# Retention and bilinear FFN on one core: the q product of slots 13, 15, 17 and 19 as eight copies each on ScalarE instead of one on GpSimd

## The chip, the cores and the metric

The kernel runs on one core of a Trainium2 chip. The metric is device time in microseconds (us) from launch to end; the lower the better. The engines are named as the profile names them: PE is TensorE (matmuls; PEld is its weight load), ACT is ScalarE, DVE is VectorE, POOL is GpSimd, and SP is SyncE, from which nearly all transfers are issued. Each engine works through its own instructions in order; between engines, semaphores say when data or a buffer is ready.

## The reference

What is computed is a retention layer (linear attention with a decay per head) followed by a bilinear feed-forward network:

```python
def _attn_ref(q, k, v):                      # (4, 8, 768, 64) each
    B, H, S, D = q.shape
    gamma = 1.0 - 2.0 ** (-5.0 - np.arange(H, dtype=np.float32))
    scale = 1.0 / np.sqrt(D)
    state = np.zeros((B, H, D, D), dtype=np.float32)
    y = np.zeros_like(q)
    for t in range(S):
        state = gamma[None, :, None, None] * state + np.einsum('bhd,bhe->bhde', k[:, :, t], v[:, :, t])
        y[:, :, t] = scale * np.einsum('bhd,bhde->bhe', q[:, :, t], state)
    return y

def _moe_ref(x, w_a, w_b, w_out):            # x: 3072 tokens x 512; w_a, w_b: 512 x 1536; w_out: 1536 x 512
    return ((x @ w_a) * (x @ w_b)) @ w_out
```

The output is float32, 3072 x 512.

## The kernel before

The 3072 tokens are cut into 24 *slots* of 128 tokens (4 batches of 6 slots). The decay is taken out of the recurrence: k of token n and head h is multiplied by a factor from a table (`ktab`), q by its inverse with the scale (`qtab`), and what is left is causal attention without a softmax, with a running state per batch. The function `scaled(eng, t, i)` makes this product for slot t, with i = 0 for k and i = 1 for q. It reads the float32 tile that a transfer has brought (`kf`, `qf`, 128 tokens x 8 heads x 64) and writes bfloat16 into the tile `kqb` of the slot. The product is one instruction of 128 x 512 (line 292), with the table's column per head broadcast over 64.

`casts(t)` prepares one of the slots 8 to 19: a new `kqb` tile, the k product, then whatever `between` holds, the q product, in slots 8 to 11 the cast of v, and then `flip(t)`, a transposing transfer issued on SP that turns `kqb` into `kqT`, followed by the loads of a later slot. q of two slots (t even and t+1) comes in one transfer. v of slots 12 to 23 is cast on ACT by `v_cast` (line 249).

Two slots after another, `turn` does the attention on PE, and the result, copied into `xt` by ACT (line 431), goes into the feed-forward network. The network runs in groups J of 2 slots (256 tokens; group 5 has 4 slots). In a *block* `ffn_ab(J, ft)` PE makes `a` (four matmuls, line 568), ACT copies it out of PSUM as `asb` (line 571), PE makes `g` (four matmuls, line 580), and DVE multiplies g by asb into `ht` (line 582). There are 12 blocks a group, numbered by ft. The PSUM banks for a and g come from a ring of three (tag "ff"), in rotation: a bank is free once its copy on ACT (an a) or its product on DVE (a g) has been made.

The output product of a group is made by a Strassen-like scheme, `Group`: its steps `p1` to `p7` (line 685) accumulate into banks A, B and C, and between steps ACT takes snapshots of A (`snaps`, line 692), before the next product goes on to add to A, and DVE adds a snapshot to B or C. The sums of `ht` that the scheme needs (`hs`, line 618) are made on POOL. `single` weaves one such group with the blocks 0, 1 and 2 of the next: p1, p7, p2, block 0, p6, block 1, p5, block 2, p3, p4. `laced` does the same for group 4 and the products of group 5 (`fa`, `fb`, with snapshots `snapf`, line 961).

The order on each engine is the order in which the program is written: `seq` chains each instruction to the one before it on its engine. The main part around the change reads, in words: slot 13 is prepared after the blocks of group 2 and before `single(2)`; slot 14 after `single(2)`; slot 15 after the blocks 3 to 5 of group 3 and before block 6; slots 16 and 17 before and after `single(3)`, slot 17 thus ahead of the casts of v of slot 14 and of the blocks 3 and 4 of group 4; slots 18 and 19 within and after group 4, slot 19 just before `laced`.

Of the kernel before, what the change touches and what calls it, by code (L numbers as in the profile page):

```python
# [31 lines left out]
def kernel(  # L32
# [10 lines left out]
    nc = tc.nc  # L43
    P = 128
    B, H, S, D = q.shape
    NCH = S // P
    HP = H // 2
# [55 lines left out]
    def seq(bi):  # L103
        ins = bi.ins
        prev = last.get(ins.engine)
        if prev is not None:
            tc.add_manual_dep(ins, prev.name, nosync, reason="program order")
        last[ins.engine] = ins
        return bi
# [7 lines left out]
    def load_slot(t, names="kqv"):  # L117
        b, ci = divmod(t, NCH)
        for nm in names:
            src = {"k": k, "q": q, "v": v}[nm]  # L120
            if nm == "q":
                if t % 2 == 0:
                    load_two(nm, src, b, ci // 2, t)
                continue
            if t % 2 == 0:
                whole[nm] = raw_tile([P, 2, H, D], F32, nm + "f", nm + "f")
            raws[nm, t] = whole[nm][:, t % 2]
            s = src[b, :, ci * P : (ci + 1) * P, :].rearrange("h p d -> p h d")
            seq(nc.sync.dma_start(out=raws[nm, t], in_=s))
# [117 lines left out]
    def cast(engine, dst, src):  # L247
        if engine is nc.scalar:
            seq(nc.scalar.copy(dst, src))
        else:  # L250
            seq(engine.tensor_copy(dst, src))  # L251
# [29 lines left out]
    def scaled(eng, t, i):  # L281
        tab = tabs[0] if i else tabs[1 if t < 2 * PAIRS else 2]
        dst, src, tab = kqb[t][:, i], raws["kq"[i], t], tab[:, t % NCH]
        if t < 2 * PAIRS:
            dst, src = (x.rearrange("p (hp r) d -> p hp r d", r=2) if x is src else x
                        for x in (dst, src))
            tab = tab.rearrange("p (hp r) o -> p hp r o", r=2).to_broadcast([P, HP, 2, D])
        else:
            dst = dst.rearrange("p hp r d -> p r hp d")
            src = src.rearrange("p (r hp) d -> p r hp d", r=2)  # L290
            tab = tab.rearrange("p (r hp) o -> p r hp o", r=2).to_broadcast([P, 2, HP, D])
        seq(eng.tensor_tensor(dst, src, tab, op=ALU.mult))  # L292

    def new_nat(t):
        kqb[t] = nat.tile([P, 2, HP, 2, D], BF16, tag="kqb", name="kqb")
        kb[t], qb[t] = kqb[t][:, 0], kqb[t][:, 1]
        vb[t] = nat.tile([P, H, D], BF16, tag="vb", name="vb")

    def casts(t, between=lambda: None):
        new_nat(t)  # L300
        scaled(nc.gpsimd, t, 0)
        between()
        scaled(nc.gpsimd, t, 1)
        if t not in range(12, 20):
            cast(nc.gpsimd, vb[t], raws["v", t])
        u = t + 2
        if u == 20:
            load_slot(u, "kq")
        flip(t)
        if u == 20:  # L310
            load_slot(u + 1, "k")
            return
        if u == 21:
            load_slot(u - 1, "v")
            load_slot(u, "v")
            load_slot(22, "kq")
            return
        if u in V_LATE:
            if u == 13:
                load_slot(12, "q")  # L320
            elif u == 19:
                load_slot(18, "kq")
            load_slot(u, {12: "k", 18: ""}.get(u, "kq"))
            if u % 2:
                load_slot(u - 1, "v")
                load_slot(u, "v")
        elif u < NSLOT:
            load_slot(u)

    def flip(t):  # L330
        if t % 2 == 0:
            kqT[t // 2] = tra.tile([P, 2, 2, HP, P], BF16, tag="kqT", name="kqT", bufs=3)
        seq(nc.sync.dma_start_transpose(
            out=kqT[t // 2][:, t % 2].rearrange("p a b c -> p (a b) c"),
            in_=kqb[t].rearrange("p a hp r d -> p (a hp r d)")))

    def late_kq(t):
        for u in (t, t + 1):
            new_nat(u)
            scaled(nc.gpsimd, u, 0)  # L340
            scaled(nc.gpsimd, u, 1)
            flip(u)
        if t == 20:
            load_slot(23, "k")
            load_slot(22, "v")
            load_slot(23, "v")
# [803 lines left out]
    ffn_out(0, 1, 1)  # L1150
    weight_sum(4)
    casts(8)
    weight_pieces(2)
    ffn_out(0, 2, 0)
# [4 lines left out]
    ffn_out(0, 3, 0)  # L1159
    ffn_out(0, 3, 1)  # L1160
    casts(9)
    weight_pieces(2)
    turn(None, 6)
    single(1, AT0, AT1, FF)
    casts(10)
    weight_pieces(4)
    casts(11)
# [101 lines left out]
```

## Time and profile before

| | before |
|---|---|
| median of 3 runs | 218.36 us (218.28 to 218.38) |
| span of the profiled execution, first to last instruction | 216.57 us |
| PE busy | 210.7 us |
| POOL busy | 154.2 us, 184 instructions |
| DVE busy | 147.5 us, 272 instructions |
| ACT busy | 104.9 us, 235 instructions |
| granted clock of PE | 1.00 |

The profile is of one execution; its span leaves out what lies before the first and after the last instruction, so the runs' times stand 1.79 us above it. In the timelines below a row gives the start and the duration in us, the engine, the line of the program, the operation, the output and the inputs by the program's names, the shape, how many instructions the row merges, and in square brackets the idle time of the engine just before, with what ended it. In the groups, the numbers behind the count are busy us, mean ns of one, and the idle time before them. In the chain of waits, shares of the span are given by the engine on which the work that ended last lay. In the rows by stage, each engine's busy time is followed by its count of instructions.

### The profile page before, as it was taken

To read this page: it belongs to the slowest core of one execution; us is meant where nothing else is said; L and a number is where in the kernel's file an instruction comes from. 1 tells how busy PE (TensorE), PEld (TensorE's weight loads), DVE (VectorE), ACT (ScalarE), POOL (GpSimd) and SP (SyncE) were. 2 spreads that over 40 slices of the span, in tenths; PEclk is the share of its full clock that TensorE was granted. 3 is DMA by queue.
4 is the path that set the end of the run, shared out by engine and by line. 5 is a ranking of instruction groups with operands and counts; after the bars stand their busy time and mean duration, and the time that the engine had idled before them with its cause. 6 is when DMAs were issued, how large, how long until landed. Compare 5 with 4: busy or idle time off the path is not lost.

```text
span 216.6 us, 5713 instructions
## 1 busy us (share of the span) xinstructions
PE 210.7 (97%) x2252; PEld 146.1 (67%) x2252; DVE 147.5 (68%) x272; ACT 104.9 (48%) x235; POOL 154.2 (71%) x184
## 2 busy tenths in 40 slices
PE   7889999999999999999999999999999999999994
PEld 3557445587458888888888877457864444458883
DVE  3777346845984486356377978676577987688962
ACT  3256325343224444464576475657546656652331
POOL 5265876879878678969869979899986999530000
PEclk9999999999999999999999999999999999999999
DMA  5999999999999999999979999950013000000055
GB/s 162 290 320 365 387 311 360 384 268 232 221 264 227 228 231 222 158 192 269 197 169 245 222 209 234 236 127 3 5 69 125 2 0 3 2 0 0 27 194 170
DMA packets 85162, 39.68 MB, mean 183 GB/s; under 512 B 57488, under 2 KB 78864, under 8 KB 85136
## 3 DMA queue, kind: packets, MB, share of 16 engines
q1 hardware_dynamic: 84992, 39.26, 76.8%
q8 instruction: 17, 0.28, 0.5%
q14 instruction: 9, 0.07, 0.1%
q10 hardware_dynamic: 144, 0.07, 0.1%
HBM read 28.31 MB, written 6.29 MB: 160 GB/s over the span
## 4 chain that ended last, share of the span: by engine, by line
PE 91%; SPq 3%; DMA 3%; POOL 0%; issue 0%; DVE 0%
PE a L568 18%; PE g L580 18%; PE mA L685 12%; PE uA L859 10%; PE mB L685 6%; PE o L605 5%; PE uB L859 5%; SPq L138 3%; DMA wsta<-in_moe_w_a_dram 3%; PE mC L685 3%; PE at L372 2%; PE uC L859 2%; PE y L420 2%; PE st L390 2%; PE fa L949 2%; PE fb L949 1%
## 5 line engine op out<-in xcount | busy, mean ns | idle before, releaser
L582 DVE TENSOR_TENSOR ht<-g,asb 128x256 bf16<-128x256 f32 (+1 forms) x70 | 34.4, 493 | 31.6 <-PE g L580 28.0
L568 PE MATMUL a<-xt,wa_bf 128*128 128x256 bf16 (+1 forms) x280 | 48.6, 300 | 0.1
L580 PE MATMUL g<-xt,wb_bf 128*128 128x256 bf16 (+1 forms) x280 | 48.4, 300 | 0.0
L571 ACT CAST asb<-a 128x256 bf16<-128x256 f32 (+1 forms) x70 | 30.0, 429 | 33.3 <-PE a L568 31.1
L580 PEld LDWEIGHTS <-wb_bf 128*128 128x128 bf16 x280 | 27.0, 98 | 10.2 <-POOL wb_bf L251 0.2
L568 PEld LDWEIGHTS <-wa_bf 128*128 128x128 bf16 x280 | 26.5, 98 | 10.7 <-POOL wa_bf L251 0.4
L292 POOL TENSOR_TENSOR kqb<-kf,ktab 128x512 bf16<-128x512 f32 x22 | 23.6, 1078 | 7.4 <-DMA kf<-in_k_dram 4.9
L866 ACT COPY snap<-uA 128x512 f32<-128x512 f32 x36 | 20.0, 588 | 15.4 <-PE uA L859 13.9
L685 PEld LDWEIGHTS <-hs 128*128 128x128 bf16 x234 | 22.8, 98 | 3.6
L378 DVE TENSOR_TENSOR aT<-at,mask 128x512 bf16<-128x512 f32 x36 | 22.3, 682 | 0.3
L292 POOL TENSOR_TENSOR kqb<-qf,qtab 128x512 bf16<-128x512 f32 x18 | 19.6, 1088 | 2.7 <-DMA qf<-in_q_dram 2.7
L618 POOL TENSOR_TENSOR ht<-gsb,asb 128x512 bf16<-128x512 bf16 x13 | 15.2, 1175 | 7.5 <-DVE gsb L618 7.4
L692 ACT COPY snaps<-mA 128x256 f32<-128x256 f32 x30 | 11.0, 374 | 18.9 <-PE mA L685 18.9
L685 PEld LDWEIGHTS <-ht 128*128 128x128 bf16 x180 | 17.5, 98 | 3.3
L618 POOL TENSOR_TENSOR hs<-ht 128x384 bf16<-128x384 bf16 (+3 forms) x14 | 15.9, 1134 | 3.5 <-DVE ht L582 3.5
L618 POOL TENSOR_TENSOR hs<-ht,hs 128x384 bf16<-128x384 bf16 (+1 forms) x17 | 16.9, 997 | 1.5 <-DVE ht L582 1.4
L685 PE MATMUL mA<-wsum,hs 128*128 128x256 bf16 x120 | 15.2, 273 | 0.0
L618 DVE TENSOR_TENSOR osb<-mB,snaps 128x256 f32<-128x256 f32 x20 | 8.4, 421 | 8.3 <-ACT snaps L692 4.4
L251 POOL CAST vb<-vf 128x512 bf16<-128x512 f32 x12 | 7.5, 641 | 6.7 <-DMA vf<-in_v_dram 6.7
L605 PE MATMUL o<-wo_bf,ht 128*128 128x512 bf16 x48 | 10.7, 379 | 0.0
L618 DVE TENSOR_TENSOR asb<-uB,snap 128x512 bf16<-128x512 f32 x12 | 8.2, 685 | 3.1 <-ACT snap L866 2.0
L618 DVE TENSOR_TENSOR gsb<-uB,snap 128x512 bf16<-128x512 f32 x12 | 8.2, 686 | 2.9 <-ACT snap L866 2.1
(138 smaller groups left out, 374.7 us busy)
## 6 DMA issues: line engine op xcount, KB each, us to landing
qf<-in_q_dram SPq DMA_DIRECT2D x12, 512.0 KB, 6.1
out_dram<-osb SPq DMA_DIRECT2D x21, 256.0 KB, 4.1
kf<-in_k_dram SPq DMA_DIRECT2D x18, 256.0 KB, 5.1
vf<-in_v_dram SPq DMA_DIRECT2D x18, 256.0 KB, 5.3
wsta<-in_moe_w_a_dram SPq DMA_DIRECT2D x6, 512.0 KB, 7.7
wsto<-in_moe_w_out_dram SPq DMA_DIRECT2D x6, 512.0 KB, 8.7
wstb<-in_moe_w_b_dram SPq DMA_DIRECT2D x5, 512.0 KB, 8.3
kf<-in_k_dram SPq DMA_DIRECT2D x3, 512.0 KB, 7.1
```

Source lines behind the costliest of these rows:

```text
L292: seq(eng.tensor_tensor(dst, src, tab, op=ALU.mult))
L378: seq(nc.vector.tensor_tensor(aT[t][:, r], at[r], mask.to_broadcast([P, HP, P]), op=ALU.mult))
L568: seq(nc.tensor.matmul(a, wa_bf[:, kt, fs], xcols(J, kt, c0, c1), start=(kt == 0), stop=(kt == KT - 1)))
L571: seq(nc.scalar.copy(asb, a))
L580: seq(nc.tensor.matmul(g, wb_bf[:, kt, fs], xcols(J, kt, c0, c1), start=(kt == 0), stop=(kt == KT - 1)))
L582: seq(nc.vector.tensor_tensor(ht[J][:, ft, c0:c1], g, asbs.pop((J, ft, c0)), op=ALU.mult))
L605: seq(nc.tensor.matmul(o, ht[J][:, ft, i * P : (i + 1) * P], wo_bf[:, ft], start=(ft == 0), stop=(ft == NFT - 1), skip_group_check=True))
L618: seq(eng.tensor_tensor(dst, x, y, op=op))
L685: seq(nc.tensor.matmul(m, w, right[:, j], start=(first and j == 0), stop=(j == NP - 1), skip_group_check=True))
L692: seq(nc.scalar.copy(self.snaps[:, n], self.bank["A"]))
L859: seq(nc.tensor.matmul(m, w, right[:, k], start=(first and k == 0), stop=(k == 1), skip_group_check=True))
L866: seq(nc.scalar.copy(self.snaps[n], self.bank["A"]))
```

## The change

`scaled` gets a branch for ACT: for each of the 8 heads one copy of 128 tokens x 64 with a factor per token, which is the head's column of the table, read from memory. `casts` calls it for q in slots 13, 15, 17 and 19; q of the other slots and all of k stay on POOL. Nothing else is edited. Four lines are inserted, so the lines behind them carry numbers higher by 4.

```diff
     def scaled(eng, t, i):
         tab = tabs[0] if i else tabs[1 if t < 2 * PAIRS else 2]
         dst, src, tab = kqb[t][:, i], raws["kq"[i], t], tab[:, t % NCH]
+        if eng is nc.scalar:
+            for h in range(H):
+                seq(nc.scalar.mul(dst[:, h % HP, h // HP, :], src[:, h, :], tab[:, h, :]))
+            return
         if t < 2 * PAIRS:
...
         new_nat(t)
         scaled(nc.gpsimd, t, 0)
         between()
-        scaled(nc.gpsimd, t, 1)
+        scaled(nc.scalar if t in (13, 15, 17, 19) else nc.gpsimd, t, 1)
         if t not in range(12, 20):
             cast(nc.gpsimd, vb[t], raws["v", t])
```

On PE, DVE and SP the instructions stand in the same order as before. The first place that matters is ACT around slot 15, between the blocks of group 3 (`asb` is a block's copy of a, `vb` a cast of v). Before:

```order
L737 COPY osb<-mA 128x256
L571 CAST asb<-a 128x256 x4
L249 CAST vb<-vf 128x512
L571 CAST asb<-a 128x256
L249 CAST vb<-vf 128x512
```

With the change:

```order
L741 COPY osb<-mA 128x256
L575 CAST asb<-a 128x256 x3
L286 ACTIVATE kqb<-qf,qtab 128x64 x8
L575 CAST asb<-a 128x256
L249 CAST vb<-vf 128x512
L575 CAST asb<-a 128x256
L249 CAST vb<-vf 128x512
```

The eight copies of slot 15 stand behind the copies of the blocks 3, 4 and 5 and ahead of that of block 6.

The second place is ACT around slot 17, at the end of `single(3)` (`mA` is bank A of the output product, `osb` the output tile). Before:

```order
L692 COPY snaps<-mA 128x256
L571 CAST asb<-a 128x256
L737 COPY osb<-mA 128x256
L249 CAST vb<-vf 128x512
L571 CAST asb<-a 128x256 x2
```

With the change:

```order
L696 COPY snaps<-mA 128x256
L575 CAST asb<-a 128x256
L741 COPY osb<-mA 128x256
L286 ACTIVATE kqb<-qf,qtab 128x64 x8
L249 CAST vb<-vf 128x512
L575 CAST asb<-a 128x256 x2
```

The eight copies of slot 17 stand ahead of the cast of v of slot 14 and of the copies of the blocks 3 and 4 of group 4. In slots 13 and 19 they stand likewise between the last block's `asb` of a group and the first snapshot of the output product that follows.

The third place is POOL, from slot 13 to slot 15. Before:

```order
L292 TENSOR_TENSOR kqb<-kf,ktab_175 128x2x4x64
L292 TENSOR_TENSOR kqb<-qf,qtab 128x2x4x64
L292 TENSOR_TENSOR kqb<-kf,ktab_175 128x2x4x64
L618 TENSOR_TENSOR wea<-wa_bf 128x2x128
L618 TENSOR_TENSOR wea<-wa_bf,wea 128x2x128
L292 TENSOR_TENSOR kqb<-qf,qtab 128x2x4x64
```

With the change:

```order
L296 TENSOR_TENSOR kqb<-kf,ktab_175 128x2x4x64 x2
L622 TENSOR_TENSOR wea<-wa_bf 128x2x128
L622 TENSOR_TENSOR wea<-wa_bf,wea 128x2x128
L296 TENSOR_TENSOR kqb<-qf,qtab 128x2x4x64
```

The q product of slot 13 is gone, and the k products of slots 13 and 14 follow each other; the q product that is left is that of slot 14.

## The prediction

> **What bounds the kernel now.** I read the page's busy row and its chain of waits first, then the busy time by stage, then the timelines of TensorE (PE) and ScalarE (ACT) at the four places that are edited.
>
> ```profile
> PE 210.7 (97%) x2252; PEld 146.1 (67%) x2252; DVE 147.5 (68%) x272; ACT 104.9 (48%) x235; POOL 154.2 (71%) x184
> PE 91%; SPq 3%; DMA 3%; POOL 0%; issue 0%; DVE 0%
> ```
>
> TensorE is busy for 97% of the span, and the chain that ended last runs through it; GpSimd (POOL), which the change relieves, holds 0% of that chain. An average can hide a stage in which POOL decides, so here are four stages around the edits (columns: stretch, length, then busy time of each engine):
>
> ```profile
> 86.00:90.00 4.00, 4.00 (x39) 3.58 (x38) 1.70 (x4) 1.71 (x6) 4.00 (x5) 1.00 0.89 188
> 90.00:98.00 8.00, 8.00 (x137) 7.02 (x136) 4.19 (x10) 4.29 (x12) 6.28 (x8) 1.00 1.35 180
> 106.00:112.00 6.00, 6.00 (x114) 5.15 (x112) 3.55 (x9) 3.71 (x10) 3.42 (x4) 1.00 0.96 149
> 118.00:122.50 4.50, 4.50 (x43) 4.03 (x42) 4.21 (x9) 2.29 (x7) 4.50 (x5) 1.00 1.09 280
> ```
>
> PE is without a gap in all four, at a granted clock of 1.00. POOL is full too in two of them, but that alone costs nothing: what counts is whether PE ever waits for it. The ends of matmuls are modelled, so I test this on their starts, in the stage of slot 15:
>
> ```profile
> 92.04 0.60 PE L568 MATMUL a<-xt,wa_bf 128*128 128x256 bf16 x4
> 92.91 0.60 PE L568 MATMUL a<-xt,wa_bf 128*128 128x256 bf16 x4
> 93.79 0.60 PE L568 MATMUL a<-xt,wa_bf 128*128 128x256 bf16 x4
> 94.22 0.60 PE L580 MATMUL g<-xt,wb_bf 128*128 128x256 bf16 x4
> 94.66 0.60 PE L568 MATMUL a<-xt,wa_bf 128*128 128x256 bf16 x4
> ```
>
> Every group of four starts 0.43 to 0.44 after the one before it (an a and its g together take 0.87 or 0.88): a steady beat with no wait in it. So relief on POOL has nothing to shorten here, and any new delay that reaches PE stays in the time, because PE has no idle time later in which to catch up.
>
> **What is removed.** Four products of q on POOL, 1.09 each by the page's group, 4.35 in all:
>
> ```profile
> L292 POOL TENSOR_TENSOR kqb<-qf,qtab 128x512 bf16<-128x512 f32 x18 | 19.6, 1088 | 2.7 <-DMA qf<-in_q_dram 2.7
> ```
>
> POOL gets ahead by about 1 us per slot, and so do the transposes that wait for it. Nobody on PE waits for that: I cost it at 0. Its cover is the beat above; without that cover it would be a gain.
>
> **What is added: the price of eight copies.** No row of before shows a 64-column ACTIVATE with a factor from memory. The nearest are three small ones at the start and the large copies later:
>
> ```profile
> 0.80 1.28 ACT L204 ACT_TABLE_LOAD   x1 [0.80 <-PEq L1253]
> 2.09 0.24 ACT L204 ACTIVATE ktab<-earg 128x48 f32<-128x48 f32 x1
> 2.24 0.32 ACT L207 ACTIVATE qtab<-earg,bq 128x48 f32<-128x48 f32 x1
> L571 ACT CAST asb<-a 128x256 bf16<-128x256 f32 x52 | 19.4, 374 | 19.9 <-PE a L568 18.4 <-DVE osb L618 0.7
> L571 ACT CAST asb<-a 128x512 bf16<-128x512 f32 x18 | 10.6, 587 | 13.4 <-PE a L568 12.6 <-issue 0.6
> ```
>
> The second ACTIVATE reads a per-token operand (bq) and takes 0.32; the first has none and takes 0.24. From 256 to 512 columns a copy grows by 213 ns, 0.83 ns a column; 16 more columns than 48 are 0.013. So one copy takes about 0.33 with its factor. The second row starts 0.15 after the first, which lasts 0.24: neighbours overlap by 0.09. **Estimate: 0.24 from start to start, 8 x 0.24 = 1.92 a slot.** From below: were the factor free, 0.24 + 0.013 - 0.09 = 0.165, 1.32 a slot. From above: without overlap 0.33, 2.65 a slot. I take 1.92, since both rows it is made of show the effect it uses (an operand from memory, two ACTIVATEs in a row). No second table load enters the built program, so the 1.28 of the first row is not paid again.
>
> **Where the copies stand.** ACT works in order, so each set of eight holds up what is behind it. Behind it are copies that empty PSUM banks, and PE cannot start a group before its bank is empty. The three "ff" banks rotate: the g of a block takes the bank of the a two groups earlier, and needs that a's copy on ACT.
>
> *Slot 15*: the eight stand between the copies of blocks 5 and 6.
>
> ```profile
> 92.68 0.37 ACT L571 CAST asb<-a 128x256 bf16<-128x256 f32 x1 [0.50 <-PE a L568]
> 93.55 0.37 ACT L571 CAST asb<-a 128x256 bf16<-128x256 f32 x1 [0.50 <-PE a L568]
> 93.82 0.62 ACT L249 CAST vb<-vf 128x512 bf16<-128x512 f32 x1
> 94.42 0.37 ACT L571 CAST asb<-a 128x256 bf16<-128x256 f32 x1
> ```
>
> A copy that follows directly starts 0.27 after an asb (93.55 to 93.82). So the eight start at 92.68 + 0.27 = 92.95 and release ACT at 94.87; the asb of block 6, due at 93.55, ends at 95.24. The a of 92.91 is block 6's; its bank goes to the g of 94.22. What ACT's end takes to reach another engine, I read here:
>
> ```profile
> 121.39 0.38 ACT L961 COPY snapf<-fb 128x256 f32<-128x256 f32 x1
> 121.84 0.42 DVE L618 TENSOR_TENSOR asb<-fa,snapf 128x256 bf16<-128x256 f32 x1 [0.25 <-ACT snapf L961]
> ```
>
> 121.84 - 121.77 = 0.07. So the g starts at 95.31 instead of 94.22: **1.09 lost**, and 0.83 of the eight is covered by ACT's idle time and the ring's slack. Late next: DVE's product of block 6 (from 95.31, 0.42, to 95.73), whose bank the a of 94.66 + 1.09 = 95.75 takes, just in time; then the casts of v and two more asb, which by the same steps arrive with PE's shifted beat. One stall, not three.
>
> *Slot 17*: here a 512-column cast of v stands between the eight and the asb.
>
> ```profile
> 106.82 0.37 ACT L737 COPY osb<-mA 128x256 f32<-128x256 f32 x1 [0.72 <-PE mA L685]
> 107.09 0.62 ACT L249 CAST vb<-vf 128x512 bf16<-128x512 f32 x1
> 107.91 0.37 ACT L571 CAST asb<-a 128x256 bf16<-128x256 f32 x1 [0.20 <-PE a L568]
> 108.58 0.60 PE L580 MATMUL g<-xt,wb_bf 128*128 128x256 bf16 x4
> ```
>
> The eight run from 107.09 to 109.01, the cast starts then, the asb 0.60 later (as 93.82 to 94.42) at 109.61 and ends at 109.98. The g of 108.58 starts at 110.05: **1.47 lost**, 0.45 covered.
>
> *Slots 13 and 19*: the eight stand before a snapshot copy, where ACT idles for long and the next product that needs the snapshot comes late.
>
> ```profile
> 83.16 0.39 ACT L571 CAST asb<-a 128x256 bf16<-128x256 f32 x1
> 83.94 0.37 ACT L692 COPY snaps<-mA 128x256 f32<-128x256 f32 x1 [0.39 <-PE mA L685]
> 85.69 0.37 ACT L571 CAST asb<-a 128x256 bf16<-128x256 f32 x1 [1.37 <-PE a L568]
> 85.93 0.82 PE L685 MATMUL mA<-wsum,hs 128*128 128x256 bf16 x6
> 118.81 0.39 ACT L571 CAST asb<-a 128x256 bf16<-128x256 f32 x1
> 119.59 0.37 ACT L692 COPY snaps<-mA 128x256 f32<-128x256 f32 x1 [0.39 <-PE mA L685]
> 121.57 0.82 PE L685 MATMUL mA<-wsum,hs 128*128 128x256 bf16 x6
> ```
>
> Slot 13: the eight run from 83.45 to 85.37, the snapshot ends at 85.74, PE may go at 85.81, and the product is due at 85.93: 0 lost, 0.12 to spare. Slot 19: 119.10 to 121.02, snapshot to 121.39, PE may go at 121.46, due at 121.57: 0 lost, 0.11 to spare. Either cover goes once eight copies take over 2.03.
>
> The factor's data is there in time. The q of an odd slot comes in the same transfer as that of the even slot before it, which POOL was working on earlier:
>
> ```profile
> 79.77 1.04 POOL L292 TENSOR_TENSOR kqb<-qf,qtab 128x512 bf16<-128x512 f32 x1 [1.41 <-DMA qf<-in_q_dram]
> 91.07 1.04 POOL L292 TENSOR_TENSOR kqb<-qf,qtab 128x512 bf16<-128x512 f32 x1
> 104.99 1.06 POOL L292 TENSOR_TENSOR kqb<-qf,qtab 128x512 bf16<-128x512 f32 x1
> 118.88 1.04 POOL L292 TENSOR_TENSOR kqb<-qf,qtab 128x512 bf16<-128x512 f32 x1
> 96.06 1.04 POOL L292 TENSOR_TENSOR kqb<-qf,qtab 128x512 bf16<-128x512 f32 x1
> ```
>
> Each of the first four lies before the 83.45, 92.95, 107.09 and 119.10 above, so no new wait on a transfer. On SP, the transposes of the odd slots now wait for ACT as well as POOL: slot 15's for 94.87, where POOL's product of q (the last row) ended at 97.10. They come no later, and are cost at 0.
>
> **Sum.** 0 + 1.09 + 1.47 + 0 = 2.56. The profiled span is 216.57 and becomes 219.13; the median of the runs, 218.36, lies 1.79 above the span, and I carry that over: **220.9**.
>
> **Rivals.**
> *No overlap.* If two copies that read their input and factor from SBUF don't overlap, eight take 2.65: slot 15 loses 1.82, slot 17 2.20, slots 13 and 19 0.61 and 0.62, in all 5.25: 223.6. Against it: the two ACTIVATEs at 2.09 and 2.24 read SBUF and overlap. For it: what follows one with an operand from memory isn't seen. [...] The trace has the 512-column cast from SBUF at 0.62, a third of my price for the eight.
>
> *The ring absorbs it* (the other side). If the copies stream at 0.107 or less, eight take 0.86 and lose 0.03 in slot 15 and 0.41 in slot 17, 0.44 in all: 218.8, and at 0.05 apiece 218.4. It decides at that price. Against it: even without a factor the rows give 0.165.
>
> *POOL's relief shows.* If a sum on POOL were what PE really waits for somewhere around the edits, up to the 4.35 could come back. For it: POOL is full in 86 to 90 and in 118 to 122.5. Against it: the beat, and PE busy to the last hundredth in these stages; the gain is bounded by PE's gaps there, some hundredths, so even with no stall from the copies it would give 218.3.
>
> **How the numbers follow.** The forecast's mechanism, with eight copies between 1.32 and 2.32: 0.82. Its ends are 2 x 1.32 - 1.28 = 1.36, so 219.7, and 3.36 + 0.29 + 0.28 = 3.93, so 222.3. No overlap: 0.08. The ring absorbs it: 0.06. POOL's relief: 0.04. The range is 219.5 to 222.4: the likeliest case with a little for the steps read to hundredths. A measurement of this kernel tells 0.2% (0.44 us) from no change: slower by more 0.90, within 0.07, faster by more 0.03.
>
> **What would show it.** In the changed trace: 32 ACTIVATEs of kqb on ACT of about 0.33 each, 0.24 apart; a hole of about 1.1 in PE before the g of block 6 after slot 15's eight, put down to ACT's asb; one of about 1.5 before the g of the second block after slot 17's; none behind slots 13 and 19; POOL at 180 instructions with more idle time. Wrong would be: PE's beat unbroken at both places (the copies are cheaper, or the ring has more slack than I count), holes behind all four (the copies are dearer), or PE catching up later, for which a wait that I don't see must exist.

## The result, and the profile after

| | before | with the change |
|---|---|---|
| median | 218.37 us (4 runs, 218.28 to 218.38) | 220.66 us (4 runs, 220.57 to 220.94) |
| ratio | | 1.011 (95% interval 1.0098 to 1.0123) |
| span of the profiled execution | 216.57 us | 218.99 us |
| ACT | 104.9 us busy, 235 instructions | 111.7 us, 267 instructions |
| POOL | 154.2 us busy, 184 instructions | 149.5 us, 180 instructions |

The change costs 2.29 us by the medians and 2.42 by the two profiled spans. From the page of the changed kernel, the busy row and the chain of waits by engine:

```profile
PE 210.8 (96%) x2252; PEld 145.9 (67%) x2252; DVE 147.7 (67%) x272; ACT 111.7 (51%) x267; POOL 149.5 (68%) x180
PE 84%; DMA 6%; SPq 5%; ACT 2%; issue 1%; POOL 1%; DVE 0%; DVEq 0%
```

PE is busy as long as before (210.8 against 210.7), in a longer span: what was added is PE's idle time. The view of who waited for whom, for PE alone, names it (total us, times, longest), and the timeline of PE shows the two places. A stretch in which PE idles is called a *hole* below:

```profile
PE g L584 <- ACT asb L575: 2.1, 2, 1.2
```

```profile
93.34 0.60 PE L584 MATMUL g<-xt,wb_bf 128*128 128x256 bf16 x4
93.78 0.60 PE L572 MATMUL a<-xt,wa_bf 128*128 128x256 bf16 x4
95.26 0.60 PE L584 MATMUL g<-xt,wb_bf 128*128 128x256 bf16 x4 [0.88 <-ACT asb L575]
95.72 0.60 PE L572 MATMUL a<-xt,wa_bf 128*128 128x256 bf16 x4
...
109.20 0.60 PE L572 MATMUL a<-xt,wa_bf 128*128 128x256 bf16 x4
110.98 0.60 PE L584 MATMUL g<-xt,wb_bf 128*128 128x256 bf16 x4 [1.18 <-ACT asb L575]
```

The beat of 0.44 is broken twice. The view counts idle time from the modelled end of the matmul before; by starts, the g of 95.26 comes 1.48 after its a, of which 0.44 is the beat: 1.04 lost. The g of 110.98 comes 1.78 after its a: 1.34 lost. Together 2.38, nearly all of the 2.42. The beat goes on after each. The g of 95.26 belongs to block 7: PE makes the blocks as a, g, a, g, the a of block 6 is that of 92.90, and its bank goes to the g three groups later, with two groups between. (The prediction's signs, and the expectation for slot 15 alone, call it the g of block 6; the time and the bank from which the prediction worked are those of this g.) The cause, in the timeline of ACT:

```profile
92.67 0.37 ACT L575 CAST asb<-a 128x256 bf16<-128x256 f32 x1 [0.50 <-PE a L572]
92.93 2.02 ACT L286 ACTIVATE kqb<-qf,qtab 128x64 bf16<-128x64 f32 x8
94.85 0.35 ACT L575 CAST asb<-a 128x256 bf16<-128x256 f32 x1
...
107.87 0.37 ACT L741 COPY osb<-mA 128x256 f32<-128x256 f32 x1 [0.72 <-PE mA L689]
108.14 2.02 ACT L286 ACTIVATE kqb<-qf,qtab 128x64 bf16<-128x64 f32 x8
110.06 0.60 ACT L249 CAST vb<-vf 128x512 bf16<-128x512 f32 x1
110.57 0.63 ACT L575 CAST asb<-a 128x256 bf16<-128x256 f32 x2
```

The asb of block 6 starts at 94.85 where it was due at 93.55; behind slot 17's eight, the first of the two asb starts at 110.57. Slots 13 and 19 have the same eight copies and no hole behind them:

```profile
83.42 2.02 ACT L286 ACTIVATE kqb<-qf,qtab 128x64 bf16<-128x64 f32 x8
85.33 0.36 ACT L696 COPY snaps<-mA 128x256 f32<-128x256 f32 x1
85.92 0.82 PE L689 MATMUL mA<-wsum,hs 128*128 128x256 bf16 x6
...
121.49 2.03 ACT L286 ACTIVATE kqb<-qf,qtab 128x64 bf16<-128x64 f32 x8
123.41 0.36 ACT L696 COPY snaps<-mA 128x256 f32<-128x256 f32 x1
123.99 0.82 PE L689 MATMUL mA<-wsum,hs 128*128 128x256 bf16 x6
```

The snapshot behind slot 13's eight ends at 85.69, and the product that needs it starts on its old time. Behind slot 19's the snapshot ends at 123.77 and the product starts at 123.99, later than its old 121.57 by the 2.42 that the holes before it cost, and by no more. One reading of the page misleads here: DMA's share of the chain, 6% where it was 3%. What is new comes from following slot 17's eight back to a transfer of v (5.40 us of the chain) that landed at 108.08, just before they start at 108.14. The row of 107.87 shows ACT at work on the output copy until then, and the eight read q, not v.

### The profile page after: what moved, and what is told of

The parts are those of the page before. It is cut to its first block, busy times and chain, and to the rows that moved or that the text cites. A ratio compares the mean times of both kernels' runs of the same rounds, so it can differ in the third digit from the quotient of the medians.

```text
span 219.0 us, 5737 instructions
## 1 busy us (share of the span) xinstructions
PE 210.8 (96%) x2252; PEld 145.9 (67%) x2252; DVE 147.7 (67%) x272; ACT 111.7 (51%) x267; POOL 149.5 (68%) x180
## 4 chain that ended last, share of the span: by engine, by line
PE 84%; DMA 6%; SPq 5%; ACT 2%; issue 1%; POOL 1%; DVE 0%; DVEq 0%
PE g L584 16%; PE a L572 16%; PE mA L689 11%; PE uA L863 9%; PE mB L689 5%; PE o L609 5%; PE uB L863 5%; SPq L138 3%; DMA wsta<-in_moe_w_a_dram 3%; PE mC L689 3%; DMA vf<-in_v_dram 2%; PE uC L863 2%; PE at L376 2%; PE y L424 2%; PE st L394 2%; PE fa L953 2%
## 5 line engine op out<-in xcount | busy, mean ns | idle before, releaser
L296 POOL TENSOR_TENSOR kqb<-kf,ktab 128x512 bf16<-128x512 f32 x22 | 23.1, 1053 | 7.2 <-DMA kf<-in_k_dram 5.8
L296 POOL TENSOR_TENSOR kqb<-qf,qtab 128x512 bf16<-128x512 f32 x14 | 15.0, 1072 | 3.4 <-DMA qf<-in_q_dram 1.8
```

## The experiments

The *cover* of a place is how long ACT may be held up there before PE waits.

### Which of the four slots costs

The first two leave some of the four q products on ACT and return the others to POOL:

```diff
-        scaled(nc.scalar if t in (13, 15, 17, 19) else nc.gpsimd, t, 1)
+        scaled(nc.scalar if t in (13, 19) else nc.gpsimd, t, 1)
```

> Only slots 13 and 19 keep their eight copies on ACT; 15 and 17 go back to POOL. My theory (the loss is PE waiting for an asb that stands behind the copies, and the cover in front of a snapshot is about 2.0 us): 0 lost, 218.4, no hole in PE. Rival A (each set of eight costs about 0.57 wherever it stands, a quarter of the 2.29 that the change lost): 219.5. Rival B (the POOL time that is given back, 2.2 us here, reaches PE): 217 to 218.

Measured: 218.28 against 218.25 in the same session, ratio 0.9999 (0.9990 to 1.0008). Two sets in covered places cost nothing, and 2 us less on POOL bring nothing.

```diff
+        scaled(nc.scalar if t in (15,) else nc.gpsimd, t, 1)
```

> Only slot 15 keeps its eight copies on ACT. My theory: PE loses the hole that the changed trace shows before the g of block 6, 1.03 to 1.05, so 219.4, and nothing else moves. Rival A (a quarter of the loss per set): 218.9.

Measured: 219.36, 1.11 more, ratio 1.0048 (1.0034 to 1.0062).

```diff
+        scaled(nc.scalar if t in (17,) else nc.gpsimd, t, 1)
```

> Only slot 17 keeps its eight copies on ACT. My theory: the second hole of the changed trace, 1.35 to 1.37, so 219.7; the losses of slots 15 and 17 add up to that of the change, 2.3 to 2.4. Rival A (a quarter of the loss per set): 218.9. Rival C (the hole of slot 17 is partly a consequence of that of slot 15, through late transfers): under 1.2, so below 219.6.

Measured: 219.58, 1.33 more, ratio 1.0060 (1.0047 to 1.0072). Each run has exactly one hole in PE put down to asb (0.9 and 1.2 by the view of waits). 1.11 and 1.33 make 2.44, against 2.29 for all four: the two places explain the whole loss, with no sign that they act on each other. A quarter per set is refuted, and so is the hole of 17 as a consequence of that of 15.

### The same work in another order

All 32 copies stay on ACT. Those of slots 15 and 17 are put into a list, and up to three leave it behind each asb (the slot's tile `kqb` is taken that much earlier):

```diff
+    def flow(n):
+        for _ in range(min(n, len(todo))):
+            seq(nc.scalar.mul(*todo.pop(0)))
...
         seq(nc.scalar.copy(asb, a))
+        flow(pace[0])
```

> All 32 copies stay on ACT, as in the change; only their order differs: those of slots 15 and 17 stand three, three and two behind the asb copies of the three blocks ahead of them, where ACT idles for 0.50 to 0.72 a block. My theory (queueing behind eight in a row): no asb comes more than 0.25 late, under the 0.30 that the ring forgives; no hole in PE, 218.4. Rival A (what counts is ACT's added work of 7 us, or what the small copies do to memory): still 220 to 220.7.

Measured: 218.33 (11 runs, 218.15 to 219.06), ratio 1.0004 (0.9996 to 1.0013): the loss is gone with all of ACT's added work still there. The timeline of ACT in this run, around slot 15:

```profile
90.93 0.37 ACT L590 CAST asb<-a 128x256 bf16<-128x256 f32 x1 [0.72 <-DVE osb L638]
91.20 0.83 ACT L285 ACTIVATE kqb<-qf,qtab 128x64 bf16<-128x64 f32 x3
91.92 0.35 ACT L590 CAST asb<-a 128x256 bf16<-128x256 f32 x1
92.17 0.83 ACT L285 ACTIVATE kqb<-qf,qtab 128x64 bf16<-128x64 f32 x3
92.90 0.36 ACT L590 CAST asb<-a 128x256 bf16<-128x256 f32 x1
93.15 0.59 ACT L285 ACTIVATE kqb<-qf,qtab 128x64 bf16<-128x64 f32 x2
93.64 0.36 ACT L590 CAST asb<-a 128x256 bf16<-128x256 f32 x1
```

The asb copies come 0.12, 0.22 and 0.09 later than before the change (91.80, 92.68, 93.55), within what the ring of three banks forgave in the change (0.26: the asb of block 6 came 1.30 late, of which PE lost 1.04); the view of PE's waits names no asb in this run.

### The cover, and the price of a copy

Slot 13 alone on ACT, with its copies made twice over:

```diff
-            for h in range(H):
+            for h in 2 * list(range(H)):
...
-        scaled(nc.scalar if t in (13, 15, 17, 19) else nc.gpsimd, t, 1)
+        scaled(nc.scalar if t in (13,) else nc.gpsimd, t, 1)
```

> Slot 13 alone goes to ACT, and its eight copies are made twice over, sixteen in a row; 15, 17 and 19 stay on POOL. My theory (slot 13 lost nothing because ACT idles and the snapshot is needed late, a cover with 0.16 to spare in the changed trace): sixteen take 3.84, of which 1.92 + 0.16 is covered, so 1.76 lost in one hole before the second product on bank A, 220.0. Rival (a snapshot's lateness never reaches PE, since the product could go on): 218.3.

Measured: 220.07 against 218.24, 1.83 more. ACT, and who PE waits for:

```profile
83.44 3.93 ACT L286 ACTIVATE kqb<-qf,qtab 128x64 bf16<-128x64 f32 x16
87.27 0.36 ACT L696 COPY snaps<-mA 128x256 f32<-128x256 f32 x1
```

```profile
PE mA L689 <- ACT snaps L696: 1.6, 1, 1.6
```

A snapshot does reach PE once it is late enough (1.6 by the view); slot 13 was free only because 1.92 just fits under its cover, which by this run is about 2.0: sixteen copies hold ACT for 3.83 (83.44 to 87.27), and 1.83 was lost.

One 512-column copy per slot without the factor, in place of the eight:

```diff
-            for h in range(H):
-                seq(nc.scalar.mul(dst[:, h % HP, h // HP, :], src[:, h, :], tab[:, h, :]))
+            seq(nc.scalar.copy(dst.rearrange("p hp r d -> p r hp d"), src.rearrange("p (r hp) d -> p r hp d", r=2)))
```

> The q product of the four slots is one 512-column copy on ACT without the factor (the factor is left out there); everything else is the change. My theory (the loss is what a set takes beyond a cover of 0.88 in slot 15 and 0.57 in slot 17): one copy takes 0.51 to 0.62, so 0 lost in slot 15 and at most 0.05 in slot 17, 218.3. Rival (any work of ACT at these places, or the hand-over of q from POOL to ACT and its waits, costs): 219 or more.

Measured: 218.27 against 218.24, ratio 1.0000 (0.9991 to 1.0010). The places and the hand-over from POOL to ACT cost nothing; the length of the set does. The timeline has the copy at

```profile
92.98 0.62 ACT L285 CAST kqb<-qf 128x512 bf16<-128x512 f32 x1
93.58 0.37 ACT L574 CAST asb<-a 128x256 bf16<-128x256 f32 x1
```

and the asb behind it only 0.03 after its old time of 93.55.

Eight copies a slot with the constant 1/8 in place of the factor:

```diff
-                seq(nc.scalar.mul(dst[:, h % HP, h // HP, :], src[:, h, :], tab[:, h, :]))
+                seq(nc.scalar.mul(dst[:, h % HP, h // HP, :], src[:, h, :], 0.125))
```

> As the change, with eight copies a slot, but each with the constant 1/8 in place of the factor from memory (the factor is left out). If the operand from memory makes a copy dearer by some 0.075 from start to start, as the two ACTIVATEs at the start of the program suggest, eight take 1.32 and lose 0.44 in slot 15 and 0.75 in slot 17: 1.19, 219.4. If the operand's reading is hidden behind the copy before, eight take 1.92 as in the change: 220.6.

Measured: 219.19 against 218.24, 0.95 more, ratio 1.0040 (1.0025 to 1.0055). The groups of ACTIVATEs by form, of the changed kernel and of this one (mean ns of one behind the busy time):

```profile
L286 ACT ACTIVATE kqb<-qf,qtab 128x64 bf16<-128x64 f32 x32 | 8.1, 343 | 0.0
```

```profile
L286 ACT ACTIVATE kqb<-qf 128x64 bf16<-128x64 f32 x32 | 5.1, 255 | 0.0
```

```profile
92.78 1.28 ACT L286 ACTIVATE kqb<-qf 128x64 bf16<-128x64 f32 x8
93.96 0.35 ACT L575 CAST asb<-a 128x256 bf16<-128x256 f32 x1
```

From the first copy to the asb behind the set it is 1.18, against 1.92 with the factor: an operand from memory costs 0.09 a copy, and eight copies without it still take twice one copy of 512 (1.18 against 0.60, 92.98 to 93.58). By covers of 0.88 and 0.58 (1.92 less the losses of 1.04 and 1.34), 1.18 should lose 0.30 and 0.60, in all 0.90: close to the 0.95. PE's timeline has both holes:

```profile
93.62 0.60 PE L572 MATMUL a<-xt,wa_bf 128*128 128x256 bf16 x4
94.37 0.60 PE L584 MATMUL g<-xt,wb_bf 128*128 128x256 bf16 x4
...
108.31 0.60 PE L572 MATMUL a<-xt,wa_bf 128*128 128x256 bf16 x4
109.35 0.60 PE L584 MATMUL g<-xt,wb_bf 128*128 128x256 bf16 x4 [0.44 <-ACT asb L575]
```

By starts, less the beat of 0.44, they are 0.31 and 0.60. In the changed kernel neighbours overlap by 0.10: 343 ns each, 240 from start to start.

### Does POOL's time matter?

The kernel before, with the four q products made twice on POOL:

```diff
-        scaled(nc.gpsimd, t, 1)
+        for _ in range(2 if t in (13, 15, 17, 19) else 1):
+            scaled(nc.gpsimd, t, 1)
```

> The kernel before, with the q product of slots 13, 15, 17 and 19 made twice over on POOL: 4.2 more on POOL, nothing on ACT. My theory (PE waits for nothing on POOL around the edits, so that neither less nor more of it by 1 us a slot shows): 218.3. Rival (POOL stands just at the edge, and the relief was hidden only because it had nothing to shorten): 218.7 to 222.

Measured: 219.32 against 218.24, 1.08 more, ratio 1.0047 (1.0032 to 1.0062): my expectation was wrong. PE's timeline has one hole:

```profile
103.13 0.49 PE L686 MATMUL mA<-wsum,hs 128*128 128x256 bf16 x3
104.17 0.50 PE L686 MATMUL mA<-wsum,hs 128*128 128x256 bf16 x3 [0.56 <-POOL hs L619]
```

A sum for single(3), which POOL makes behind slot 15, comes too late for the fourth of the six matmuls that use it. By starts this hole is 0.71, less than the 1.08 of the medians: in the traced execution PE came to this place 0.22 late already, an offset that it has from its first 40 us on, and 0.22 and 0.71 make the 0.93 by which its span is longer. To settle the place, the doubling was split into slots 13 and 15, and slots 17 and 19:

> The q product is made twice on POOL in slots 13 and 15 only. The run with all four twice showed a hole of 0.72 in PE before the fourth product with the sum hs2 of single(3), which POOL makes right behind slot 15. My theory (that place alone is the edge, with about 0.9 to spare in the kernel before): the same hole here, 219.0 to 219.3. Rival (each extra product adds a quarter of the 1.08): 218.8.

Measured: 219.39 against 218.28, 1.11 more, ratio 1.0053 (1.0038 to 1.0068), with the same hole (0.91 by the view, POOL's hs).

> The q product is made twice on POOL in slots 17 and 19 only. My theory (the edge lies at single(3) alone, ahead of slot 17, and behind slot 17 POOL waits 1.97 for DVE anyway): 0 lost, 218.3. Rival (a quarter of the 1.08 for each): 218.8.

Measured: 218.38, ratio 1.0005 (0.9995 to 1.0014). So POOL has an edge at one place, single(3), and its room there is under the 2.1 of two products. In the kernel before, POOL's sum and the matmuls that use it stood so:

```profile
100.52 1.79 POOL L618 TENSOR_TENSOR hs<-ht,hs 128x384 bf16<-128x384 bf16 x2
102.91 0.82 PE L685 MATMUL mA<-wsum,hs 128*128 128x256 bf16 x6
```

The sum ended at 102.31 and the fourth matmul started at 103.24 (102.91 and three steps of 0.11), 0.93 later. With all four products doubled, the sum ended 1.80 later, at 104.11:

```profile
102.33 1.78 POOL L619 TENSOR_TENSOR hs<-ht,hs 128x384 bf16<-128x384 bf16 x2
```

The laced order, with the k products of the same slots made twice instead, so that POOL's work is again as before:

```diff
-        scaled(nc.gpsimd, t, 0)
+        for _ in range(2 if t in (13, 15, 17, 19) else 1):
+            scaled(nc.gpsimd, t, 0)
```

> The laced order, with all 32 copies on ACT, and the k product of the same four slots made twice over on POOL, so that POOL has as much to do as in the kernel before. My theory (the relief is real room on POOL, which nothing uses): 218.3, no hole at single(3), where the same doubling without the relief cost 1.08. Rival (what hurts in a doubled product isn't POOL's time but the later transposes): 219 or more.

Measured: 219.59, 1.31 more, ratio 1.0058 (1.0043 to 1.0073). That is neither theory's mechanism. No hole stands at single(3); the only one ends at 93.39, is put down to asb, and is 0.91 by starts (the traced execution is the fastest of the four, 219.27):

```profile
92.04 0.60 PE L588 MATMUL a<-xt,wa_bf 128*128 128x256 bf16 x4
93.39 0.60 PE L601 MATMUL g<-xt,wb_bf 128*128 128x256 bf16 x4 [0.75 <-ACT asb L591]
```

ACT's timeline says why:

```profile
90.93 0.37 ACT L591 CAST asb<-a 128x256 bf16<-128x256 f32 x1 [0.72 <-DVE osb L639]
92.26 0.83 ACT L285 ACTIVATE kqb<-qf,qtab 128x64 bf16<-128x64 f32 x3 [0.96 <-DMA qf<-in_q_dram]
92.99 0.35 ACT L591 CAST asb<-a 128x256 bf16<-128x256 f32 x1
```

The laced copies stand 1.7 earlier than the eight did, and here q of slots 14 and 15 had not landed. By the trace's landings it came at 92.15 in this run, 90.73 in the first laced run and 89.47 in the kernel before. To test that, slot 15 went back to POOL, and k was made twice only in slots 13, 17 and 19:

> As the run before, but q of slot 15 goes back to POOL: slots 13 and 19 (eight in a row) and 17 (three, three, two) stay on ACT, and the k product is made twice in those three slots, so that POOL's work is again as in the kernel before. In the run before, the three copies behind the asb of block 3 waited 0.96 for the transfer of q of slots 14 and 15, and PE's only hole followed. My theory (that wait is the whole of its 1.3, and the doubled k products cost nothing where the q products left room): 218.3. Rival (the doubled k products cost by themselves): 219 or more.

Measured: 218.26 against 218.25, ratio 1.0000 (0.9991 to 1.0009), no hole in PE. The doubled k products cost nothing in the room that the q products left, so the loss of the run before hangs on slot 15's early copies. Whether doubling k has a part in q's late landing there stays open (see the last section). No version was faster than the kernel before.

## Why the prediction was right

- **What bounds it**: right. PE had no idle time in which to catch up; both holes stand in the end time (2.38 of the 2.42).
- **POOL's relief at 0**: right as a number (laced, with all four products gone from POOL, 218.33). The reason given, that nobody on PE waits for POOL, was thinner than it sounded: POOL's 0% of the chain is not a margin, and 2 us more ahead of single(3) cost 1.1.
- **The price, 0.24 from start to start, 1.92 a slot**: measured 0.24 ((2.02 - 0.34) / 7) and 1.92 (92.93 to 94.85). Each copy lasts 0.34 where I had 0.33, and neighbours overlap by 0.10 where I had 0.09; that these two errors of a hundredth cancel is luck. The difference that I read from the two small ACTIVATEs put the operand at 0.075; it is 0.09.
- **Slot 15, 1.09**: measured 1.04, and 1.11 by itself in the run times. The g that waits is block 7's, not block 6's as the signs have it; the bank was the right one. The steps behind it (DVE, the next a) came just in time, as worked out: the a starts at 95.72, 0.46 after the g, where the beat is 0.44.
- **Slot 17, 1.47**: measured 1.34. The term that was too large is the cast of v: I took 0.60 from it to the next asb, from a row in which that asb was waiting for PE; when nothing else holds the asb it is 0.51 (110.06 to 110.57). That is 0.09 of the 0.13; the rest is hundredths in the other steps.
- **Slots 13 and 19, 0**: right, with a spare of about 0.16 in slot 13; a set twice as long lost 1.83.
- **Transfers and transposes at 0**: right for the change. The eight copies of slot 15 start 2.4 after q's landing in its trace (90.48). The lead is not large: in the doubled laced run the copies stood 1.7 earlier, q landed 1.7 later, and they waited.
- **Sum**: 2.56 forecast, 2.42 by the spans, 2.29 by the medians. The rival without overlap fell (neighbours overlap by 0.10), and so did the one in which the ring absorbs the sets (two holes) and the one in which POOL's relief shows (218.28 and 218.33 without the holes).

## What to carry to other kernels

An engine that is busy half the time (ACT here, 48% of the span) has no free room by that share alone: work put in its queue delays what stands behind it, and here its cost was the length of the set less the cover at that place (1.92 less 0.88 and 0.58 in slots 15 and 17; nothing in slot 13, with a cover of about 2.0), so it must be worked out place by place, from the next copy that frees a PSUM bank. If such work must go there, lace it between the copies: here threes of 0.72 (91.20 to 91.92) at places where ACT had idled for 0.50 to 0.72 cost nothing (218.33). Check that its data has landed by then: where q had not, 1.31 was lost. An engine that is absent from the chain of waits may still be within a microsecond of it (POOL here, 0% of the chain and 0.93 ahead of PE at single(3)): doubling its work in one place is a cheap way to see how far off it is.

## What had not been expected of the hardware

The same kind of transfer, 512 KB of q for slots 14 and 15, was issued between 83.4 and 85.3 in all the traces here and landed between 89.14 and 92.86, a spread of 3.7. From issue to landing it took 5.7 to 6.7 in eleven traces and 7.6 to 8.3 in three. Those three, which also landed last, are of the doubled laced run (92.15), of the run with the q products of slots 17 and 19 made twice (92.58), which does the same as the kernel before up to that point, and of the last run (92.86), where nothing on ACT or PE hung on it. What makes it late was not found: k of slot 13 is doubled in two of the three, but not in the third. All four executions of the doubled laced run took 219.27 or more, which fits a late landing in each, but only one of them has a trace; and one of eleven executions of the first laced run took 219.06, which may be the same thing and wasn't shown either.
